# A fused attention and two-layer MoE kernel: another order of VectorE and ScalarE work in its chunk pairs, relu taken with the addition out of PSUM, and weight subtractions on GpSimd

## The chip, the cores and the metric

The kernel runs on one core of a Trainium2 chip. The metric is the device time of one execution in microseconds (us): the median of several runs. A core has five engines that each take their instructions strictly in order: TensorE (PE; its weight loads are shown apart as PEld), VectorE (DVE), ScalarE (ACT), GpSimd (POOL) and SyncE (SP), which here only starts transfers.

## The reference, cut to what matters

Attention over clusters comes first; its output, 1536 tokens of 512 values, goes through two dense layers with 2048 hidden values each. The change concerns the two layers.

```python
def _moe_ref(x, w_in, w_out):
    h = x @ w_in
    g = h * (1.0 / (1.0 + np.exp(-1.702 * h)))
    return (g @ w_out).astype(np.float32)

def _moe2_ref(x, w_in, w_out):
    h = x @ w_in
    r = np.maximum(h, 0.0)
    g = r * r
    return (g @ w_out).astype(np.float32)

    # reference: q, k, v are (2, 8, 768, 64), the weights 64-bit floats
    x = np.ascontiguousarray(attn_out.transpose(0, 2, 1, 3)).reshape(B * S, H * D)
    x = _moe_ref(x=x, **moe_kwargs)
    return _moe2_ref(x=x, **moe2_kwargs)
```

## The kernel before, in words

**Numbers.** Every matrix operand is split into a high part (a ScalarE cast to the short matmul format) and a low part (the rest, by a VectorE subtraction), and a product is three products of parts: high by high, high by low, low by high. The weights arrive as 64-bit floats and are decoded into 32-bit ones: ScalarE takes the magnitude of the high word (L81), then VectorE does four instructions, L90, L92, L95 and L98 (`decode`); the last two read two tiles each. `parts` (L102) splits a decoded weight tile into `hi` and `lo`.

**Order.** The program's order is written out by hand (`manual_schedule`): each engine executes its instructions in the order in which the code issues them, and an instruction that waits holds back everything behind it on its engine.

**Attention** takes the first 300 us and a little more. Towards its end the first weights of layer 0 are decoded beside it. Each head group ends in a normalization by GpSimd (L501, 128x768).

**Chunk loop** (L884 to L941): layer 0 for the first batch half, 16 chunks of 128 hidden values. For each chunk TensorE does `hidden` (into PSUM tile `ph`) and then `second` of the chunk before (into `y`). Beside this, the next chunk's two weight tiles (`wi` from w_in, `oh`/`ol` from w_out) are loaded, decoded and split. Two raw tiles alternate between w_in and w_out: a new load (L72, L75) can start only when the last decoding step has read the raw tile. The decoded weights are also stored in DRAM (`keep`, L122) for the second batch half.

**Chunk pairs** (L951 to L1071): 24 of them in three passes of eight: layer 0 for the second batch half, layer 1 for the first, layer 1 for the second. Each pair multiplies a block of two chunks and carries `second` of the pair before in four quarters (`pend[0]` to `pend[3]`). The first three pairs are plain: four units, each with a product into PSUM (L839), a gate (sigmoid on ScalarE, multiplication on VectorE, L701), a cast `gh` (L982) and a subtraction `gl` (L984). The other 21 do seven products of sums in place of eight (L832). TensorE's order in these is: B11, B21, `pend[0]`, T2, T1, `pend[1]`, T3, B22, `pend[2]`, T4, `pend[3]`. Two PSUM tiles alternate, so T1 needs the first addition (L1016) done, T4 the additions L1045 and L1047, and the next pair's second product the gate behind T4. Between them VectorE and ScalarE prepare the next pair's weights: `sums` (four additions or subtractions, L799 to L802), `early` (casts L805 and subtractions L806 of `wxh`/`wxl`), `late` (`wyh`/`wyl`). At pass boundaries the combinations of the tokens (`Combos.sum`, L776, and `Combos.part`, L783 and L784) and the copies of finished outputs (`finish`, L747) come on top.

**Layer 1's weights** are decoded inside the pairs of the first two passes, up to four tiles per pair by the table `COUNTS`; `do(i, steps)` places steps 0 to 3 (the four decoding instructions) and 4 (storing or splitting) of the pair's i-th tile. In layer 1 the gate is `gated` (L710, a maximum and a multiplication in one VectorE instruction) or, for the last quarter, a ScalarE relu and a VectorE multiplication (L703, L704); then a cast (L695) and a subtraction (L696).

Of the kernel before, what the change touches and what calls it, by code (L numbers as in the profile page):

```python
# [20 lines left out]
BIG = float(2**40)  # L21

# [9 lines left out]
def tile_kernel(ctx, tc, q, k, v, cent, w_in1, w_out1, w_in2, w_out2, cw_cols, out):  # L32
# [665 lines left out]
    def gate(layer, dst, src, tmp):  # L698
        if layer == 0:
            nc.scalar.activation(tmp, src, ACTF.Sigmoid, scale=1.702)  # L700
            nc.vector.tensor_mul(dst, src, tmp)  # L701
        else:
            nc.scalar.activation(tmp, src, ACTF.Relu)  # L703
            nc.vector.tensor_mul(dst, tmp, tmp)  # L704

    def gated(layer, dst, tmp):
        if layer == 0:
            gate(layer, dst, dst, tmp)
        else:
# [76 lines left out]
    class Weights:  # L786
# [56 lines left out]
    COUNTS = (2, 4, 4, 2, 2, 2, 2, 1, 1, 2, 2, 2, 2, 2, 2, 0)  # L843
# [17 lines left out]
    def step(k):  # L861
# [22 lines left out]
    for fc in range(KF):  # L884
# [15 lines left out]
        def act(i):  # L900
            gate(0, s[:, cut[i]], first[i] if fc == 0 else hidden(xs, w, i), s[:, cut[i]])
# [49 lines left out]
    for q, (layer, b, p) in enumerate(slots):  # L951
# [22 lines left out]
        if q < NC:  # L974
            xq = [[x[i] for i in r] for r in ((0, 1), (7, 6))]
            for c, g in ((0, ga), (1, gb)):
                for i, at in enumerate((lo_, hi_)):
                    plain(bank[i], wq.x, c, xq[i])
                    gate(0, h[:, c, at], bank[i], s[:, at])
                    if 2 * c + i < n:  # L980
                        absolute()
                    nc.scalar.copy(g[0][:, at], h[:, c, at])  # L982
                    do(2 * c + i, (0, 1))
                    nc.vector.tensor_sub(g[1][:, at], h[:, c, at], f32(g[0][:, at]))  # L984
                    do(2 * c + i, (2, 3, 4))
                    if i:
# [122 lines left out]
```

## Time and profile before

| | us |
|---|---|
| median of 3 runs | 814.11 (812.75 to 814.85) |
| the profiled execution | 813.53 |
| its span in the trace | 811.7 |
| TensorE busy | 784.2, 97% |
| VectorE busy | 666.0, 82% |
| ScalarE busy | 478.2, 59% |
| GpSimd busy | 121.9, 15% |

The span runs from the first to the last instruction that the profiler recorded. Busy shares are means over stages with different limits; which wait ends last in a stage is read from the stage's own rows. A timeline row has its start in us, its length, engine, line, operation, output and input tile with shapes, a count where equal ones are taken together, and in brackets how long the engine stood idle before it and what ended that. TensorE's granted clock is given as a share of its upper level: 1.00 is 2.4 GHz, 0.50 is 1.2 GHz.

### The profile page before, as it was taken

The numbers are of one execution on the slowest core, as the hardware profiler recorded it, in microseconds if no ns is written. First come the engines' busy times: TensorE is split into PE (matmuls) and PEld (weight loads), VectorE is DVE, ScalarE is ACT, GpSimd is POOL, SyncE is SP. The second block draws the span as 40 slices with busy tenths as digits, with TensorE's granted clock in tenths as the row PEclk, the third lists the DMA queues.
The fourth block names the chain that finished last, engine by engine and source line by source line (L and its number), as shares of the span: only waits on it lengthen the run. The fifth ranks groups of instructions, "written<-read, shape, count | busy, mean of one in ns | idle before, by whom it ended". The sixth has DMA issues, their size and how long they took to land.

```text
span 811.7 us, 12557 instructions
## 1 busy us (share of the span) xinstructions
PE 784.2 (97%) x4521; PEld 697.9 (86%) x4521; DVE 666.0 (82%) x1202; ACT 478.2 (59%) x1004; POOL 121.9 (15%) x121
## 2 busy tenths in 40 slices
PE   8999999999999999999999899989999999999997
PEld 5898889999988887788899789977998887998986
DVE  7899999998898787878888898888888987656653
ACT  5898888988988644444564545556354545433331
POOL 1444435545436100000000000000000000000000
PEclk9999999999999999999999899999999999999999
DMA  8342533532311344445436533312342301300002
GB/s 229 89 132 63 160 105 90 138 89 66 83 26 34 88 153 142 149 142 178 157 107 205 155 92 116 131 53 64 118 155 80 104 26 40 117 27 26 27 1 78
DMA packets 48478, 81.87 MB, mean 101 GB/s; under 512 B 5120, under 2 KB 32544, under 8 KB 48416
## 3 DMA queue, kind: packets, MB, share of 16 engines
q1 hardware_dynamic: 43232, 73.96, 30.5%
q10 hardware_dynamic: 5184, 7.12, 2.7%
q8 instruction: 35, 0.57, 0.3%
q14 instruction: 27, 0.22, 0.1%
HBM read 58.76 MB, written 11.58 MB: 87 GB/s over the span
## 4 chain that ended last, share of the span: by engine, by line
PE 52%; DVE 27%; ACT 10%; DMA 5%; issue 4%; POOL 1%; ACTq 0%; SPq 0%; DVEq 0%; POOLq 0%
PE ps L832 12%; PE y L727 12%; PE pa L453 5%; PE pt L428 5%; DMA raw<-in_moe_w_in_dram 4%; PE ph L140 4%; PE y L721 3%; PE ps L404 3%; DVE el L441 3%; DVE dec L98 2%; DVE nm L410 2%; PE ps L405 2%; DVE dec L95 2%; DVE wxl L806 2%; PE y L723 2%
## 5 line engine op out<-in xcount | busy, mean ns | idle before, releaser
L695 ACT CAST gh<-h 128x384 fp32r<-128x384 f32 (+1 forms) x63 | 39.1, 621 | 109.9 <-DVE h L710 82.2
L441 DVE TENSOR_TENSOR el<-pt,eh 128x384 fp32r<-128x384 f32 x192 | 97.5, 549 | 7.6 <-ACT eh L438 7.3
L410 DVE TENSOR_REDUCE nm<-ps 128x1 f32<-128x768 f32 x96 | 91.2, 950 | 11.9 <-PE ps L405 11.0
L419 ACT ACTIVATE e<-ps,nm 128x768 f32<-128x768 f32 x96 | 88.7, 924 | 16.9 <-DVE nm L410 9.6
L438 ACT CAST eh<-pt 128x384 fp32r<-128x384 f32 x192 | 84.2, 497 | 8.5 <-PE pt L428 7.5
L428 PE MATMUL pt<-identF,e 128*128 128x128 f32 x576 | 82.2, 276 | 3.3 <-DVE el L441 2.8
L832 PE MATMUL ps<-x,wxh 128*128 128x384 f32 x336 | 74.4, 343 | 5.5 <-ACT wxh L805 2.9
L727 PE MATMUL y<-oh,gl 128*128 128x512 f32 x192 | 75.9, 395 | 0.0
L727 PE MATMUL y<-ol,gh 128*128 128x512 f32 x192 | 75.8, 395 | 0.0
L727 PE MATMUL y<-oh,gh 128*128 128x512 f32 x192 | 74.6, 389 | 0.0
L428 PEld LDWEIGHTS pt<-identF,e 128*128 128x128 f32 x576 | 64.4, 140 | 9.6 <-DVE el L441 8.9
L404 PE MATMUL ps<-k,q 80*128 80x512 f32 x192 | 70.3, 366 | 0.5 <-ACT k L371 0.5
L696 DVE TENSOR_TENSOR gl<-h,gh 128x384 fp32r<-128x384 f32 (+1 forms) x63 | 43.5, 691 | 32.7 <-ACT gh L695 32.7
L81 ACT ACTIVATE dec<-raw 128x512 f32<-128x512 f32 x64 | 43.1, 673 | 45.0 <-DMA raw<-in_moe_w_out_dram 15.9
L832 PEld LDWEIGHTS ps<-x,wxh 128*128 128x128 f32 x336 | 59.9, 191 | 11.0 <-ACT wxh L805 3.2
L405 PE MATMUL ps<-k,q 128*128 128x512 f32 x192 | 61.2, 340 | 0.0
L832 PE MATMUL ps<-x,wyh 128*128 128x384 f32 x252 | 55.3, 340 | 5.7 <-DVE h L1045 5.1
L140 PE MATMUL ph<-xh,wi 128*128 128x512 f32 (+1 forms) x256 | 53.7, 342 | 3.3 <-ACT wi L104 3.1
L832 PEld LDWEIGHTS ps<-x,wyh 128*128 128x128 f32 x252 | 44.0, 188 | 11.5 <-DVE h L1045 4.4
L140 PEld LDWEIGHTS ph<-xh,wi 128*128 128x128 f32 x256 | 41.4, 189 | 12.1 <-ACT wi L104 6.6
L721 PE MATMUL y<-gh,ol 128*128 128x512 f32 x128 | 51.0, 399 | 0.0
L721 PE MATMUL y<-gl,oh 128*128 128x512 f32 x128 | 50.8, 397 | 0.0
(170 smaller groups left out, 1896.0 us busy)
## 6 DMA issues: line engine op xcount, KB each, us to landing
raw<-in_moe_w_in_dram SPq DMA_DIRECT2D x32, 512.0 KB, 4.0
raw<-in_moe_w_out_dram SPq DMA_DIRECT2D x32, 512.0 KB, 3.2
wb<-wst SPq DMA_DIRECT2D x24, 512.0 KB, 4.6
wst<-dec SPq DMA_DIRECT2D x32, 256.0 KB, 2.5
k<-k SPq DMA_DIRECT2D x16, 192.0 KB, 4.0
q<-q SPq DMA_DIRECT2D x16, 192.0 KB, 2.9
rr<-row SPq DMA_DIRECT2D x16, 192.0 KB, 3.6
out_dram<-o SPq DMA_DIRECT2D x12, 256.0 KB, 2.0
```

The costliest lines, as they stand in the source:

```text
L140: nc.tensor.matmul(ph, w[:, kc * P:(kc + 1) * P], xs[kc][z][:, a:a + n], start=(j == 0), stop=(j == len(terms) - 1))
L404: nc.tensor.matmul(ps[:, a:a + n], q1[0:K1, qs], k1[0:K1, a:a + n], start=True, stop=False)
L405: nc.tensor.matmul(ps[:, a:a + n], q2[:, qs], k2[:, a:a + n], start=False, stop=True)
L410: nc.vector.tensor_reduce(out=nm, in_=live["s", t][:, 0:S], op=ALU.max, axis=AX, negate=True)
L419: nc.scalar.activation(e, live["s", t][:, 0:S], ACTF.Exp, bias=live.pop(("nm", t)), accum_out=sums[:, s:s + 1])
L428: nc.tensor.transpose(pt[:, i], e[:, kc * P:(kc + 1) * P], identF)
L438: nc.scalar.copy(place("eh", t, u), live["pt", t, u])
L441: nc.vector.tensor_tensor(out=place("el", t, u), in0=live.pop(("pt", t, u)), in1=f32(place("eh", t, u)), op=ALU.subtract)
L696: nc.vector.tensor_sub(gl[:, at], src[:, at], f32(gh[:, at]))
L721: nc.tensor.matmul(y[m], l[:, cs], r[:, 0:512], start=first, stop=last)
L727: nc.tensor.matmul(y[m], l[:, m * P:(m + 1) * P], r, start=(fc == 0 and z == 0), stop=(fc == KF - 1 and z == 2))
L832: nc.tensor.matmul(ps, w[a][:, wi, kc * P:(kc + 1) * P], x[z][:, kc, :], start=start and j == kc == 0, stop=j == 2 and kc == 1, skip_group ...
```

## The change

1. `parts` does its subtraction on GpSimd, but for the w_out tiles of layer 1, which stay on VectorE.
2. In layer 1 the addition out of PSUM, the maximum with 0 and a minimum with the largest float are one VectorE instruction (`TENSOR_ADD_SAT`, in `total`). ScalarE then squares twice (`squared`): once into the high part, once in place; VectorE subtracts (`low`).
3. In a pair, the additions stand ahead of the next weights' `sums`, and the second half of `early` comes behind the last gate or at the pair's end. The combinations of tokens have other places (`EXTRA` for the plain pairs).
4. `COUNTS` changes: the first and third pair 2 and 4 become 3 and 3; the eighth pair does no decoding (1 before), the sixteenth one (0 before).

```diff
-    def parts(tf, hi, lo):
+    def parts(tf, hi, lo, engine=nc.gpsimd):
         nc.scalar.copy(hi, tf)
-        nc.vector.tensor_tensor(out=lo, in0=tf, in1=f32(hi), op=ALU.subtract)
+        engine.tensor_tensor(out=lo, in0=tf, in1=f32(hi), op=ALU.subtract)
...
+    def total(layer, dst, ps, other):
+
         if layer == 0:
+            nc.vector.tensor_tensor(out=dst, in0=ps, in1=other, op=ALU.add)
         else:
+            nc.vector._custom_dve(TENSOR_ADD_SAT, out=dst, in0=ps, in1=other, s0=TOP, s1=0.0)
+
+    def low(g, c, at):
+        nc.vector.tensor_sub(g[1][:, at], h[:, c, at], f32(g[0][:, at]))
+
+    def squared(g, c, at):
+        nc.scalar.activation(g[0][:, at], h[:, c, at], ACTF.Square)
+        nc.scalar.activation(h[:, c, at], h[:, c, at], ACTF.Square)
...
-    COUNTS = (2, 4, 4, 2, 2, 2, 2, 1, 1, 2, 2, 2, 2, 2, 2, 0)
+    COUNTS = (3, 4, 3, 2, 2, 2, 2, 0, 1, 2, 2, 2, 2, 2, 2, 1)
+    EXTRA = ((((0, 0),), ((0, 1),)), (((0, 2), (1, 4)), ((0, 3), (1, 2))), (((1, 5),), ()))
...
-                parts(tf, *wo2[fc])
+                parts(tf, *wo2[fc], nc.vector)
...
-        nc.vector.tensor_tensor(out=h[:, 0, lo_], in0=B_, in1=p1, op=ALU.add)
-        do(0, (0, 1))
-        gated(layer, h[:, 0, lo_], s[:, lo_])
+        total(layer, h[:, 0, lo_], B_, p1)
+        if layer == 0:
+            nc.scalar.activation(s[:, lo_], h[:, 0, lo_], ACTF.Sigmoid, scale=1.702)
+            do(0, (0, 1))
+            nc.vector.tensor_mul(h[:, 0, lo_], h[:, 0, lo_], s[:, lo_])
+            nc.scalar.copy(ga[0][:, lo_], h[:, 0, lo_])
+        else:
+            squared(ga, 0, lo_)
+            do(0, (0, 1))
...
-        if q + 1 < len(slots):
-            wn.sums()
-            wn.early()
+        if more:
+            wn.early(0)
...
-        nc.vector.tensor_tensor(out=h[:, 1, lo_], in0=B_, in1=u2, op=ALU.add)
-        do(1, (2, 3))
-        gated(layer, h[:, 1, :], s)
-        do(1, (4,))
-        split(gb, h[:, 1, :])
+        total(layer, h[:, 1, lo_], B_, u2)
+        if layer == 0:
+            nc.scalar.activation(s, h[:, 1, :], ACTF.Sigmoid, scale=1.702)
+            if more:
+                wn.sums()
+            nc.vector.tensor_mul(h[:, 1, :], h[:, 1, :], s)
+            nc.scalar.copy(gb[0], h[:, 1, :])
+        else:
+            squared(gb, 1, slice(0, S))
+            if more:
+                wn.sums()
+        do(1, (2,))
+        low(gb, 1, slice(0, S))
...
+        if more and n < 2:
+            wn.early(1)
+        do(1, (3,))
+        low(ga, 0, hi_)
+        if more and n > 1:
+            wn.early(1)
+        do(1, (4,))
```

The rows below are instructions in the order in which an engine takes them. VectorE in the chunk loop, one chunk, before (`s` is the gate, `wi` and `ol` the low parts of the two weight tiles, `dec` the decoded tile):

```order
L701 TENSOR_TENSOR s<-ph,s 128x256
L105 TENSOR_TENSOR wi<-dec,wi 128x512
L95 SCALAR_TENSOR_TENSOR dec<-raw_5025,dec 128x512
L696 TENSOR_TENSOR gl<-s,gh 128x256
L98 SCALAR_TENSOR_TENSOR dec<-raw_5025,dec 128x512
L105 TENSOR_TENSOR ol<-dec,oh 128x512
L90 TENSOR_SCALAR dec<-dec 128x512
L92 TENSOR_SCALAR dec<-dec 128x512
L95 SCALAR_TENSOR_TENSOR dec<-raw_5066,dec 128x512
L98 SCALAR_TENSOR_TENSOR dec<-raw_5066,dec 128x512
```

The same place after the change:

```order
L699 TENSOR_TENSOR gl<-s,gh 128x512
L703 TENSOR_TENSOR s<-ph,s 128x256
L98 SCALAR_TENSOR_TENSOR dec<-raw_5025,dec 128x512
L699 TENSOR_TENSOR gl<-s,gh 128x256
L101 SCALAR_TENSOR_TENSOR dec<-raw_5025,dec 128x512
L93 TENSOR_SCALAR dec<-dec 128x512
L95 TENSOR_SCALAR dec<-dec 128x512
L98 SCALAR_TENSOR_TENSOR dec<-raw_5066,dec 128x512
L101 SCALAR_TENSOR_TENSOR dec<-raw_5066,dec 128x512
```

The two subtractions have left VectorE; the lines are three further down in the changed file, so that L98 and L101 there are the two last decoding steps.

GpSimd in the loop's first chunks after the change (before, it took only the normalization, the last row of L501):

```order
L108 TENSOR_TENSOR wi<-dec,wi 128x512
L108 TENSOR_TENSOR ol<-dec,oh 128x512
L108 TENSOR_TENSOR wi<-dec,wi 128x512
L108 TENSOR_TENSOR ol<-dec,oh 128x512
L504 TENSOR_TENSOR x_1_86<-x_1_86,rr 128x768
L108 TENSOR_TENSOR wi<-dec,wi 128x512
L108 TENSOR_TENSOR ol<-dec,oh 128x512
```

GpSimd has two subtractions for each chunk now, and the last head group's normalization (L504 there) stands behind the fourth `ol`, inside the loop.

VectorE in the first plain pair, from the second unit's gate to the next pair's weights, before (`h` is a unit's gate):

```order
L776 TENSOR_TENSOR x_1_86<-x_1_86 128x2x384
L701 TENSOR_TENSOR h<-ps,s 128x384
L984 TENSOR_TENSOR gl<-h,gh 128x384
L701 TENSOR_TENSOR h<-ps,s 128x384
L984 TENSOR_TENSOR gl<-h,gh 128x384
L806 TENSOR_TENSOR wxl<-wb,wxh 128x512
```

After:

```order
L783 TENSOR_TENSOR x_1_86<-x_1_86 128x2x384
L703 TENSOR_TENSOR h<-ps,s 128x384
L93 TENSOR_SCALAR dec<-dec 128x512
L95 TENSOR_SCALAR dec<-dec 128x512
L713 TENSOR_TENSOR gl<-h,gh 128x384
L98 SCALAR_TENSOR_TENSOR dec<-raw_5328,dec 128x512
L101 SCALAR_TENSOR_TENSOR dec<-raw_5328,dec 128x512
L703 TENSOR_TENSOR h<-ps,s 128x384
L713 TENSOR_TENSOR gl<-h,gh 128x384
L813 TENSOR_TENSOR wxl<-wb,wxh 128x512
```

A whole decode (L93, L95, L98, L101) now stands between the third unit's gate and the fourth's.

VectorE in the first pair of the last pass, from a token part to the additions in front of T4, before (`o` is a finished output):

```order
L784 TENSOR_TENSOR x_7587<-x_0_85,x_7586 128x768
L799 TENSOR_TENSOR wt<-wb 128x256
L800 TENSOR_TENSOR wt<-wb,wt 128x256
L801 TENSOR_TENSOR wt<-wb 128x256
L802 TENSOR_TENSOR wt<-wb,wt 128x256
L806 TENSOR_TENSOR wxl<-wb,wxh 128x512
L806 TENSOR_TENSOR wxl<-wt,wxh 128x512
L784 TENSOR_TENSOR x_7589<-x_1_86,x_7588 128x768
L747 COPY o<-y_6717 128x512
L1045 TENSOR_TENSOR h<-ps,p_4018 128x384
```

After:

```order
L791 TENSOR_TENSOR x_7590<-x_0_85,x_7589 128x768
L791 TENSOR_TENSOR x_7586<-x_1_86,x_7585 128x768
L813 TENSOR_TENSOR wxl<-wb,wxh 128x512
L754 COPY o<-y_6705 128x512
L710 ISA h<-ps,p_4018 128x384
L710 ISA h<-ps,p_5033 128x384
L806 TENSOR_TENSOR wt<-wb 128x256
L807 TENSOR_TENSOR wt<-wb,wt 128x256
L808 TENSOR_TENSOR wt<-wb 128x256
L809 TENSOR_TENSOR wt<-wb,wt 128x256
```

The four sums and the second subtraction of `wxl` no longer stand in front of the additions, which are the custom instruction (ISA, L710) there.

## Rows read from the trace of the kernel before

**Rows 1.** Page, part 1: busy us, share, instructions of each engine.

```profile
PE 784.2 (97%) x4521; PEld 697.9 (86%) x4521; DVE 666.0 (82%) x1202; ACT 478.2 (59%) x1004; POOL 121.9 (15%) x121
```

**Rows 2.** TensorE's waits from 300 us: us in total, times, longest us.

```profile
PE ps L832 <- DVE h L1045: 5.1, 5, 1.7
PE ph L140 <- ACT wi L104: 3.1, 4, 1.7
PE ps L832 <- ACT wxh L805: 2.9, 1, 2.9
PE ps L832 <- DVE h L1016: 1.5, 3, 0.6
...
PE ps L832 <- DVE wxl L806: 0.5, 1, 0.5
```

**Rows 3.** TensorE's timeline: two chunk starts, the first plain pair's start.

```profile
297.71 0.40 PE L140 MATMUL ph<-xh,wi 128*128 128x512 f32 x1
...
306.13 0.40 PE L140 MATMUL ph<-xh,wi 128*128 128x512 f32 x1
...
404.64 0.34 PE L839 MATMUL ps<-x,wxh 128*128 128x384 f32 x1
```

**Rows 4.** TensorE's timeline: starts of chunk pairs.

```profile
417.46 0.44 PE L839 MATMUL ps<-x,wxh 128*128 128x384 f32 x1 [0.18 <-DVE h L701]
...
453.88 0.69 PE L832 MATMUL ps<-x,wxh 128*128 128x384 f32 x1 [2.85 <-ACT wxh L805]
...
490.44 0.34 PE L832 MATMUL ps<-x,wxh 128*128 128x384 f32 x1
...
506.05 0.34 PE L832 MATMUL ps<-x,wxh 128*128 128x384 f32 x1
...
522.39 0.34 PE L832 MATMUL ps<-x,wxh 128*128 128x384 f32 x1
...
559.53 0.34 PE L832 MATMUL ps<-x,wxh 128*128 128x384 f32 x1
...
689.39 0.51 PE L832 MATMUL ps<-x,wxh 128*128 128x384 f32 x2
...
705.10 0.33 PE L832 MATMUL ps<-x,wxh 128*128 128x384 f32 x1
```

**Rows 5.** Busy us by engine (instructions), PEclk, DMA share, GB/s, one stretch.

```profile
core 0: us, PE busy (x) PEld busy (x) DVE busy (x) ACT busy (x) POOL busy (x), PEclk, DMA share, GB/s
453.90:460.50 6.60, 6.12 (x18) 5.32 (x19) 6.53 (x13) 4.35 (x8) 0.00 (x0) 0.50 0.94 302
```

**Rows 6.** Timelines of ScalarE and VectorE in one chunk.

```profile
346.45 0.66 ACT L81 ACTIVATE dec<-raw 128x512 f32<-128x512 f32 x1 [1.99 <-DMA raw<-in_moe_w_in_dram]
...
347.66 0.69 DVE L105 TENSOR_TENSOR ol<-dec,oh 128x512 fp32r<-128x512 f32 x1 [1.50 <-ACT oh L104]
...
349.91 0.69 DVE L98 SCALAR_TENSOR_TENSOR dec<-raw,dec 128x512 uint32<-128x512 uint32 x1
```

**Rows 7.** Timelines of GpSimd and VectorE in attention.

```profile
126.11 1.01 POOL L385 TENSOR_TENSOR v<-rawv,v 128x384 fp32r<-128x384 f32 x1
126.30 1.36 DVE L98 SCALAR_TENSOR_TENSOR dec<-raw,dec 128x512 uint32<-128x512 uint32 x1
...
253.65 1.83 POOL L501 TENSOR_TENSOR x<-x,rr 128x768 f32<-128x768 f32 x1
```

**Rows 8.** VectorE's timeline: gates in the first and third plain pair.

```profile
415.26 0.55 DVE L701 TENSOR_TENSOR h<-ps,s 128x384 f32<-128x384 f32 x1
...
449.16 0.55 DVE L701 TENSOR_TENSOR h<-ps,s 128x384 f32<-128x384 f32 x1
...
452.21 0.55 DVE L701 TENSOR_TENSOR h<-ps,s 128x384 f32<-128x384 f32 x1
```

**Rows 9.** VectorE's timeline: first pair of the last pass.

```profile
681.36 0.42 DVE L799 TENSOR_TENSOR wt<-wb 128x256 f32<-128x256 f32 x1
...
685.50 0.55 DVE L1045 TENSOR_TENSOR h<-ps,p 128x384 f32<-128x384 f32 x1
```

**Rows 10.** Page, part 5: ScalarE's casts of gates, busy us, mean ns.

```profile
L695 ACT CAST gh<-h 128x384 fp32r<-128x384 f32 (+1 forms) x63 | 39.1, 621 | 109.9 <-DVE h L710 82.2
```

More of the change, by code (lines that the diff above doesn't have):

```diff
@@ L8 @@
 from concourse._compat import with_exitstack
+from concourse.dve_ops import TENSOR_ADD_SAT
 from concourse.masks import make_identity
@@ L21 @@
 BIG = float(2**40)
+TOP = float(np.finfo(np.float32).max)
 E_LO = float(np.uint32(0x38000000).view(np.float32))
@@ L900, in act @@
         def act(i):
-            gate(0, s[:, cut[i]], first[i] if fc == 0 else hidden(xs, w, i), s[:, cut[i]])
+            gate(s[:, cut[i]], first[i] if fc == 0 else hidden(xs, w, i), s[:, cut[i]])
         act(0)
@@ L991, in tile_kernel @@
                             wn.plain(c, wq.x)
-                            combos.sum(2 * q + c)
                         elif not c:
                             wn.sums()
-                            combos.part(4)
                         else:
-                            wn.early()
-                            combos.part(2)
+                            wn.early(0)
+                            wn.early(1)
+                        for kind, j in EXTRA[q][c]:
+                            (combos.part if kind else combos.sum)(j)
+                    do(u, (4,))
             wo = wo1
@@ L1004, in tile_kernel @@
             continue
+        last = p == NP - 1 and q + 1 < len(slots)
+        more = q + 1 < len(slots)
         product(A, wq.x, wq.B11, x[Combos.A11], True)
@@ L1041, in tile_kernel @@
         do(1, (0, 1))
-        if p == NP - 1 and q + 1 < len(slots):
-            nxt.part(2)
         product(A, wq.y, wq.T3, x[Combos.S3])
-        nc.vector.tensor_tensor(out=h[:, 1, hi_], in0=A, in1=p5, op=ALU.add)
+        total(layer, h[:, 1, hi_], A, p5)
         product(B_, wq.y, wq.B22, x[Combos.S4])
-        nc.vector.tensor_tensor(out=h[:, 1, lo_], in0=B_, in1=u2, op=ALU.add)
-        do(1, (2, 3))
-        gated(layer, h[:, 1, :], s)
-        do(1, (4,))
-        split(gb, h[:, 1, :])
+        total(layer, h[:, 1, lo_], B_, u2)
[5 more added lines that the diff above has]
+            nc.scalar.copy(gb[0], h[:, 1, :])
+        else:
+            squared(gb, 1, slice(0, S))
[3 more added lines that the diff above has]
+        low(gb, 1, slice(0, S))
+        if last:
+            nxt.part(3)
         pend[2]()
@@ L1054, in tile_kernel @@
         product(A, wq.y, wq.T4, x[Combos.A22])
-        gate(layer, h[:, 0, hi_], A, s[:, hi_])
-        split(ga, h[:, 0, :], hi_)
+        if layer == 0:
+            gate(h[:, 0, hi_], A, s[:, hi_])
+            nc.scalar.copy(ga[0][:, hi_], h[:, 0, hi_])
+        else:
+            nc.scalar.activation(h[:, 0, hi_], A, ACTF.Relu)
+            squared(ga, 0, hi_)
+        if more and n < 2:
[3 more added lines that the diff above has]
+        if more and n > 1:
+            wn.early(1)
+        do(1, (4,))
         if q < 2 * NP and p > 3:
@@ L1060, in tile_kernel @@
             nxt.sum(p - 4)
-        if p == NP - 1 and q + 1 < len(slots):
-            nxt.part(3)
+        if last:
             nxt.part(4)
```

56 lines of the change are left out of this document (25 added, 31 removed).

## The prediction

> **What bounds the kernel now.** Three views, in this order. The page's engine shares first [rows 1]: TensorE is busy 97% of the span, VectorE 82%, ScalarE 59%, GpSimd 15%. The change leaves TensorE's instructions as they are, so all that can be won is the time in which it stands or runs at half clock. Then its waits from 300 us on [rows 2]: VectorE's adds and ScalarE's casts are what it waits for. Last, the starts of its groups, which tell what a stretch loses against the same stretch undisturbed; I count by these, since a halted TensorE loses more than the wait that is written beside it.
>
> - Chunk loop [rows 3]: one chunk without a stall takes 306.13 − 297.71 = 8.42. The eleven up to 404.64 take 98.51 against 92.62: 5.9 lost.
> - Chunk pairs [rows 4]: layer 0 takes 506.05 − 490.44 = 15.61 per undisturbed pair, layer 1 705.10 − 689.39 = 15.71. Against these: the opening loses 2.85 ahead of 453.88 and then 36.56 − 31.22 = 5.34 up to 490.44. Of that 5.34, 3.3 is the clock: from 453.9 to 460.5, right behind the 2.85 in which TensorE stood, the granted clock is 0.50, the lower of its levels [rows 5], so half of 6.6 us went. Then 0.73 (506.05 to 522.39, 16.34 long), 5.92 (522.39 to 559.53, two pairs with the first pass boundary), and 4.18 (559.53 to 689.39, eight pairs with the second boundary). Behind 689.39 nothing is lost.
>
> So some 19 us are lost in the pairs and 5.9 in the chunk loop. The profiled run was 813.53, its span 811.7 (1.8 lies outside the span); the median of the runs shown is 814.11, 0.6 above. The sum is made against 813.53.
>
> **Part 1: the subtraction of `parts` goes from VectorE to GpSimd.** What sets the chunk's period is a ring [rows 6]: a raw tile lands, ScalarE takes its magnitude at 346.45, casts `oh`, VectorE waits for that cast and subtracts (347.66), decodes in four instructions until 349.91 + 0.69 = 350.60, and the raw tile is free for its next load. With the subtraction gone from VectorE, L90 and L92 can start when the magnitude is done (346.45 + 0.66 = 347.11) and end at about 348.0; before they ended near 349.1. But GpSimd then subtracts beside VectorE. In attention a decode's L98 that began at 126.30 took 1.36, not its usual 0.69, beside a GpSimd subtraction of 1.01 that ended at 127.12, and was done 0.54 after that end [rows 7]. GpSimd takes 1.01 for 384 columns and 1.83 for 768, so some 1.28 for 512 (estimate, by line between the two). If it starts at 348.0, it holds until 349.3; L95 is done 0.55 later at 349.85, L98 0.7 later at 350.55: the same as the 350.60 of before. Price per chunk: 0, between −0.7 (no hindrance: VectorE is freed of the 0.69) and +1.3 (the whole GpSimd time comes on top). I take 0, since the row of 126.30 is the same instruction against the same kind of neighbour.
>
> The Trainium skill ("SBUF — State Buffer", section "Who interferes with whom") says that a VectorE instruction with two SBUF inputs contends with a GpSimd instruction that reads SBUF, and that the one which issues first holds the shared pair for its whole length while the other fully blocks. The row at 126.30 agrees that the hindrance ends with the GpSimd instruction; taken literally the waiting instruction would then need all of its 0.69 where the row shows 0.54, and the sum would be 0.15 × 11 = 1.7 higher.
>
> One instruction more is moved by this: GpSimd's 128x768 normalization of the last head group (L501), which ran beside attention's end, now stands behind the fourth `ol` subtraction, so it falls into the loop, between L95 and L98 of a chunk. It takes 1.83 [rows 7]: cost between 0 (falls where VectorE waits) and 1.84. I take **+1.0**, the middle, there being no row for it.
>
> **Part 2: opening, plain pairs.** Counts of decodes in the first pairs go from 2, 4, 4 to 3, 4, 3. A plain unit with a decode takes VectorE 452.21 − 449.16 = 3.05 from its gate to the next [rows 8]. The first pair's third unit (gate at 415.26) now carries one, so the fourth unit's gate starts at 415.26 + 3.05 = 418.31 and ends at 418.86. The next pair's second product needs it and started at 417.46 [rows 4]: about **+1.4**, a new stall. The third pair loses a decode behind its last gate but starts 1.4 later; its last gate lands near 453.5 where it was 452.21, and the pair's casts and the first product behind it near 455.2. So the stall of 2.85 stays about as long, and with it the clock's 3.3. What goes is behind it: the 0.5 for `wxl` [rows 2], and 1.5, the rest of the 5.34 (5.34 − 3.3 − 0.5), waits for adds that no longer stand behind the sums and casts of the next weights. Together +1.4 − 0.5 − 1.5 = **−0.6**.
>
> **Part 3: order within a pair.** Before, four sums and both halves of `wxl` stand ahead of the adds (L1045, L1047) on VectorE; in the last pass's first pair 4.14 us lie between the first sum at 681.36 and the add at 685.50, and TensorE waits for the add [rows 9]. Now the sums stand behind the adds and the second half of `wxl` behind the gate. They are the same instructions, covered by the fourth product and the fourth quarter of `second`; without that cover they would cost their length, at 0.42 a sum 1.7. The 5.1 on L1045 and 1.5 on L1016 [rows 2] thus go: **−0.7** (506.05), **−5.9** at the first boundary. At that boundary one thing is late next: with no decode in the pair ahead, `gl` of the last quarter stands behind ScalarE's cast and VectorE's second `wxl`, some 1.3 later than before, and the next pair's first quarter reads it: I leave **+1.1** there (0 to 1.3). Layer 1 with its boundary gets **−4.0** of the 4.18; 0.2 is kept for the same wait.
>
> The decode that leaves the eighth pair for the sixteenth, and the x-combinations taken earlier, cost nothing on VectorE: it is 82% busy, and behind 522.39 it has the sums' room; without it, one decode is 2.25 (from 347.66 + 0.69 to 350.60 [rows 6]).
>
> **Part 4: relu with the add, squares on ScalarE.** No row shows the new add (add, max 0, min). It reads PSUM and SBUF like the add of 0.55 at 685.50 [rows 9]; the bounds are 0.42, a sum of 256 columns, and 1.36, the slowest decode row [rows 7]. I take 0.55, the same operands. At the upper bound three adds cost a pair 2.4 more, of which VectorE gets back the three multiplies that it loses, so even then nothing is late by more than some tenths. ScalarE does two squares where VectorE did one instruction and ScalarE one cast; the cast is 0.62 [rows 10], 39 us for 63. One more per group: covered, ScalarE being 59% busy; uncovered it would be 0.6 on the wait for `gl`, again inside the +0.2 and the rival below. Cost 0.
>
> **Sum.** 0 + 1.0 − 0.6 − 0.7 − 5.9 + 1.1 − 4.0 = −9.1, so 813.53 − 9.1 = **804.4**.
>
> **Rivals.**
> - *GpSimd's subtractions don't hinder VectorE.* Then VectorE's ring is 0.7 shorter per chunk, TensorE's 8.42 becomes the period, the 5.9 of the loop goes, and the normalization's 1.0 does too: 804.4 − 6.9 = 797.5. For it: only one instruction pair of the trace is against it. Against: that row is the very decode step that the ring ends with. 0.17.
> - *Slower: GpSimd lengthens the ring.* If each subtraction (1.28, two per chunk, of which one on the ring) comes on top of the decode instead of beside the wait, eleven chunks pay 1.28 each: +14.1, 818.5. It outweighs the gain of 10.1 elsewhere once a chunk's ring grows by more than 0.9. For it: two of the four decode steps read two tiles as the hindered L98 did. Against: ahead of 347.66 VectorE stood for 1.50 [rows 6], time that the new order hands back. 0.11.
> - *The stalls of the pairs only move*: to `gl` behind the second `wxl`, and to ScalarE's squares. If half of the 9.6 gained at the boundaries and in layer 1 comes back, 809.2. For it: TensorE takes products and `second` in a fixed order and four buffers of `gh`/`gl` leave little room. Against: VectorE's and ScalarE's idle time. 0.14.
> - *The opening's stall shortens enough that the clock stays at its upper level.* Then 3.3 more goes: 801.1. For it: a decode less in the third pair; against: the 1.4 lost ahead. 0.14.
> - Forecast 0.40; anything else 0.04.
>
> **How the numbers follow.** A measurement of this kernel can tell about 0.3%, 2.4 us, from no change. Faster: forecast, first, third and fourth rival, less the third's upper tail and the unknown rest: 0.79. Within: 0.10, from the third's tail and smaller forms of the second. Slower: 0.11. The range takes in the first rival's 797.5 with a us for the unknown add, and the third's 809.2 with 1.8 for the unhidden norm: 796.5 to 811.0; left out are the slower rival and most of the rest.
>
> **What would show it.** In the changed profile: a wait of about 1.6 on the fourth gate ahead of the second plain pair; one of about 2.9 with a clock of 0.50 behind it near 455; no wait above 0.3 on the adds at the boundaries, about 1.1 on `gl` at layer 1's first pair; L98 rows of 1.3 to 1.4 beside GpSimd rows near 1.28; the eleven chunks 98 to 101 long. The prediction is wrong if the chunks take less than 95 or more than 103, or if a boundary still loses over 2.

## The result and the profile after

The changed kernel takes 802.25 us (median of 4 runs, 800.09 to 803.57) against 814.48 for the kernel before on the same chip (812.75 to 816.35): a ratio of 0.9847, 95% interval 0.9816 to 0.9878. The profiled execution took 803.57, its span is 800.6. The forecast of 804.4 and its range held, but several of its steps were wrong, and errors of both signs cancelled: that the sum came so near is in part luck.

The engines' shares of the changed kernel, as in [rows 1]:

```profile
PE 778.6 (97%) x4520; PEld 697.6 (87%) x4521; DVE 645.2 (81%) x1122; ACT 507.5 (63%) x1052; POOL 163.7 (20%) x153
```

VectorE gave up 20.8 us of busy time, ScalarE took 29.3 more, GpSimd 41.8 more. That tells little yet; the waits and the starts do. TensorE's waits from 290 us on (as [rows 2]: us in total, times, longest):

```profile
PE ph L143 <- ACT wi L107: 3.4, 4, 1.5
PE ps L840 <- ACT wxh L812: 2.7, 1, 2.7
PE ps L847 <- DVE h L703: 2.4, 1, 2.4
PE y L728 <- DVE gl L713: 0.9, 1, 0.9
PE ps L840 <- DVE h L710: 0.6, 1, 0.6
```

The waits of 5.1 and 1.5 for additions are down to 0.6 (L710); those for the loop's cast (3.4) and for `wxh` (2.7) are as they were; the 2.4 on the gate L703 is new. TensorE's starts, answering to [rows 3, 4] with the places in the same order; ahead of them is the start of the chunk that stood at 280.87 before (two chunks of 8.42 ahead of 297.71):

```profile
279.02 0.40 PE L143 MATMUL ph<-xh,wi 128*128 128x512 f32 x1
...
402.81 0.34 PE L847 MATMUL ps<-x,wxh 128*128 128x384 f32 x1
...
417.81 0.44 PE L847 MATMUL ps<-x,wxh 128*128 128x384 f32 x1 [2.36 <-DVE h L703]
...
454.09 0.69 PE L840 MATMUL ps<-x,wxh 128*128 128x384 f32 x1 [2.72 <-ACT wxh L812]
...
486.76 0.34 PE L840 MATMUL ps<-x,wxh 128*128 128x384 f32 x1
...
502.36 0.34 PE L840 MATMUL ps<-x,wxh 128*128 128x384 f32 x1
...
517.96 0.34 PE L840 MATMUL ps<-x,wxh 128*128 128x384 f32 x1
...
551.49 0.34 PE L840 MATMUL ps<-x,wxh 128*128 128x384 f32 x1
...
678.25 0.33 PE L840 MATMUL ps<-x,wxh 128*128 128x384 f32 x1
```

Differences of neighbouring starts, in us, for all kernels that were run. The columns: **start** of that chunk; the **14 chunks** from it to the first plain pair; the three **plain** pairs; the two pairs behind, **opening**; the next **two** pairs; **boundary 1** with the eighth and ninth pair; the eight pairs of **layer 1** with the second boundary. Undisturbed, the 14 chunks would take 14 × 8.42 = 117.88, opening, two and boundary 1 31.22 each, and layer 1 125.68. (Attention's last products end at 268.97 in the kernel before, and not at 300.)

| kernel | start | 14 chunks | plain | opening | two | boundary 1 | layer 1 |
|---|---|---|---|---|---|---|---|
| before | 280.87 | 123.77 | 49.24 | 36.56 | 31.95 | 37.14 | 129.86 |
| changed | 279.02 | 123.79 | 51.28 | 32.67 | 31.20 | 33.53 | 126.76 |
| e1_parts_vector | 281.16 | 122.84 | 51.94 | 31.34 | 31.20 | 33.52 | 126.76 |
| e2_loop_vector | 279.45 | 125.64 | 51.95 | 31.34 | 31.21 | 33.53 | 126.75 |
| e3_norm_early | 278.14 | 122.44 | 51.50 | 32.87 | 31.20 | 33.54 | 126.75 |
| e4_memset | 278.64 | 117.88 | 51.99 | 31.35 | 31.20 | 33.52 | 126.76 |
| e5_old_counts | 278.90 | 124.51 | 49.13 | 34.54 | 31.20 | 37.32 | 125.63 |
| e6_old_relu | 278.09 | 125.79 | 51.69 | 31.37 | 31.20 | 34.11 | 130.75 |
| e7_before_relu | 281.89 | 122.40 | 49.15 | 37.03 | 31.91 | 36.51 | 128.54 |
| e8_counts_243 | 280.07 | 125.57 | 49.14 | 32.77 | 31.20 | 36.27 | 126.78 |
| e9_before_parts | 278.50 | 123.96 | 49.50 | 37.26 | 31.93 | 37.21 | 129.90 |
| e10_before_counts | 280.22 | 123.48 | 51.90 | 33.22 | 31.91 | 36.18 | 130.79 |
| e11_ol_later | 278.71 | 118.42 | 51.82 | 31.36 | 31.20 | 33.51 | 126.75 |
| e12_ol_later_counts | 279.97 | 118.00 | 48.94 | 32.88 | 31.20 | 33.54 | 126.74 |

The span became 11.1 shorter: 1.85 in attention, 0 in the chunks, 1.85 in plain pairs and opening together, 0.75, 3.61 and 3.10. The last columns repeat to some hundredths wherever the code is the same; the 14 chunks do not. The same loop took 123.8 to 125.8 in five kernels, so a difference under 2 us there is not read from one profile.

Some entries hold a stretch in which TensorE's clock was granted at 0.50 to 0.51 for some 3.5 us; each such stretch costs 1.7. There is one in the plain pairs or the opening of every row (in the opening of before, e5, e7 and e9 it is twice as long and costs 3.4), one in boundary 1 of e5 and of e8, one in layer 1 of e6, and one in attention, near 21 us, in e2, e7, e8 and e12. Where one of them bears on a comparison, it is said there.

### The profile page after: what moved, and what is told of

It is laid out like the page before. It is cut to its first block, busy times and chain, and to the rows that moved or that the text cites. A ratio compares the mean times of both kernels' runs of the same rounds, so it can differ in the third digit from the quotient of the medians.

```text
span 800.6 us, 12533 instructions
## 1 busy us (share of the span) xinstructions
PE 778.6 (97%) x4520; PEld 697.6 (87%) x4521; DVE 645.2 (81%) x1122; ACT 507.5 (63%) x1052; POOL 163.7 (20%) x153
## 4 chain that ended last, share of the span: by engine, by line
PE 58%; DVE 17%; DMA 12%; ACT 8%; issue 2%; POOL 1%; ACTq 0%; SPq 0%; POOLq 0%; DVEq 0%
PE ps L840 16%; PE y L734 15%; DMA raw<-in_moe_w_in_dram 6%; PE pa L456 5%; PE pt L431 5%; DMA raw<-in_moe_w_out_dram 3%; PE y L728 3%; PE ps L407 3%; DVE el L444 3%; PE ps L408 2%; DVE dec L98 2%; DVE nm L413 2%; DVE dec L101 2%; ACT dec L84 2%; DMA wst<-dec 2%
## 5 line engine op out<-in xcount | busy, mean ns | idle before, releaser
L716 ACT ACTIVATE gh<-h 128x384 fp32r<-128x384 f32 (+1 forms) x48 | 30.4, 633 | 72.5 <-DVE h L710 72.0
L98 DVE SCALAR_TENSOR_TENSOR dec<-raw,dec 128x512 uint32<-128x512 uint32 x64 | 70.0, 1093 | 0.8
L713 DVE TENSOR_TENSOR gl<-h,gh 128x384 fp32r<-128x384 f32 (+1 forms) x75 | 50.0, 667 | 22.9 <-ACT h L717 19.6
```

Source lines behind the costliest of these rows:

```text
L98: nc.vector.scalar_tensor_tensor(out=t, in0=high, scalar=0xC0000000, in1=t, op0=ALU.bitwise_and, op1=ALU.bitwise_or)
```

## The experiments: GpSimd's subtractions

**All subtractions back on VectorE** (e1)

```diff
-    def parts(tf, hi, lo, engine=nc.gpsimd):
+    def parts(tf, hi, lo, engine=nc.vector):
```

> The changed kernel with every subtraction of parts back on VectorE. Theory: GpSimd's subtractions gain only in attention, where VectorE no longer stands 0.81 us for ScalarE's cast ahead of its own subtraction, twice; so attention is about 1.9 longer again (chunk loop from 297.7 where the changed kernel has 295.9), the sixteen chunks behind it stay near 107 us, and the time is near 804.2. Rival: the chunk loop was helped by GpSimd; then it is 2 or more longer than 107 and the time over 805. Other rival: the loop was hurt; then it is below 105 and the time under 802.

Measured: 803.88 us, ratio to before 0.988 (0.9865 to 0.9895). The chunk starts at 281.16, 2.1 later than in the changed kernel, and the 14 chunks take 122.84, within the loop's own spread. Attention's part of the theory holds; the loop gained nothing from GpSimd.

**Only the loop's on VectorE (e2); and GpSimd's subtractions alone in the kernel before (e9)**

```diff
-            parts(tf, new[0], new[1])
+            parts(tf, new[0], new[1], nc.vector)
...
-                parts(tf, new[2], new[3])
+                parts(tf, new[2], new[3], nc.vector)
```

> The changed kernel with the subtractions of the chunk loop back on VectorE and only the two inside attention on GpSimd. Theory: attention as in the changed kernel (loop stretch begins near 295.9), the loop stretch 106.9 as in both kernels, time near 802.3. Rival, that GpSimd's subtractions hurt the loop: 105 or less, 800.5. Rival, that they helped: 109 or more.

The other run takes item 1 of the change, and nothing else, into the kernel before:

```diff
-    def parts(tf, hi, lo):
+    def parts(tf, hi, lo, engine=nc.gpsimd):
...
-        nc.vector.tensor_tensor(out=lo, in0=tf, in1=f32(hi), op=ALU.subtract)
+        engine.tensor_tensor(out=lo, in0=tf, in1=f32(hi), op=ALU.subtract)
...
-                parts(tf, *wo2[fc])
+                parts(tf, *wo2[fc], nc.vector)
```

> The kernel before with only the subtractions of parts put on GpSimd. Theory: attention about 1.9 shorter, the loop stretch unchanged at 106.9 though L95 of the decoding rises from 0.69 to about 1.65, everything behind it as before: 812.5. Rival: loop helped, under 810; loop hurt, over 814.

Measured: 802.75 (ratio 0.9858, 0.9838 to 0.9878) and 812.27 (0.998, 0.9968 to 0.9993), so the subtractions alone are worth some 2 us of the 12, and that is in attention. The loop took 123.96 in e9, where the kernel before takes 123.77. Over all kernels, the start is 278.1 to 280.1 (mean 278.9, ten kernels) where attention's two subtractions are on GpSimd and 280.2 to 281.9 (mean 281.0, four kernels) where they are on VectorE: 2.1 us. Without the 1.7 that the clock cost e2, e7, e8 and e12 ahead of it, it is 277.7 to 279.0 against 280.2 to 281.2, and the two groups stand well apart.

VectorE's timeline in attention shows why, first of the kernel before, then of the changed one:

```profile
64.13 0.34 DVE L258 CAST nat<-rawk 128x384 fp32r<-128x384 f32 x1
65.28 0.82 DVE L105 TENSOR_TENSOR wi<-dec,wi 128x512 fp32r<-128x512 f32 x1 [0.81 <-ACT wi L104]
66.03 0.94 DVE L410 TENSOR_REDUCE nm<-ps 128x1 f32<-128x768 f32 x1
```

```profile
64.15 0.34 DVE L261 CAST nat<-rawk 128x384 fp32r<-128x384 f32 x1
64.44 0.96 DVE L413 TENSOR_REDUCE nm<-ps 128x1 f32<-128x768 f32 x1
```

Before, VectorE stood 0.81 for ScalarE's cast, then subtracted, and the row maximum queued behind it began at 66.03, not 64.44. Some 1.2 of that reached TensorE, and the same happens once more near 98 us (with `ol`); 0.4 of the two is lost again near 205 us.

**The normalization ahead of the loop** (e3)

```diff
-            if c == 4:
+            if c == 1:
                 last_norm()
```

> The changed kernel with the last 128x768 normalization issued behind the first ol subtraction, so that GpSimd does it near 276, ahead of the loop's critical stretch. Theory: the 2.22 us of one decode step beside it (0.69 usual) falls to 0.69 and the stretch from the chunk start at 295.9 to the first plain pair is 1.5 shorter: 105.4, time near 800.7. Rival: the loop makes it up elsewhere, no change, 802.3.

In the changed kernel the normalization falls on the decode of one chunk, VectorE's and GpSimd's rows:

```profile
300.82 2.29 POOL L504 TENSOR_TENSOR x<-x,rr 128x768 f32<-128x768 f32 x1
301.44 2.22 DVE L101 SCALAR_TENSOR_TENSOR dec<-raw,dec 128x512 uint32<-128x512 uint32 x1
```

Moved ahead (it runs at 273.92), the same step takes 0.69 and the 14 chunks 122.44 against 123.8 to 125.8. The time is 801.61 (0.9852, 0.9835 to 0.987): by the intervals not apart from the changed kernel. The 1.5 is there in the rows, and the stretch agrees with it, but the time does not settle it. The starts of single chunks do. TensorE stands ahead of the chunk behind that step, and the third of the 14 chunks takes 9.9 in place of 8.42:

```profile
295.86 0.40 PE L143 MATMUL ph<-xh,wi 128*128 128x512 f32 x1
...
305.76 0.50 PE L143 MATMUL ph<-xh,wi 128*128 128x512 f32 x1 [1.31 <-ACT wi L107]
```

It took 9.9 to 10.2 in all five kernels that have the normalization there and the subtractions on GpSimd, and 8.4 to 8.8 in the nine others. The eleven chunks behind it took 97.9 on average in those five, and 98.0 in the five kernels with the loop's subtractions on VectorE in their old place. So the normalization costs 1.5 beside these subtractions, and by these averages the subtractions themselves neither gain nor lose.

**A fill in place of the loop's subtraction** (e4)

```diff
+        if engine is None:
+            nc.gpsimd.memset(f32(lo), 0.0)
+            return
         engine.tensor_tensor(out=lo, in0=tf, in1=f32(hi), op=ALU.subtract)
...
-            parts(tf, new[0], new[1])
+            parts(tf, new[0], new[1], None)
```

The loop's other calls of `parts` get the same `None`; the kernel so leaves the low parts of these weights out.

> The changed kernel with the loop's GpSimd subtractions replaced by a GpSimd fill of the same tile, which reads nothing; the low parts of layer 0's first weights are left out of the computation. Theory: the fill does not hold up VectorE, L98 falls from 1.65 to 0.69, each chunk's ring from 8.5 to about 7.6, below TensorE's 8.42, and the loop stretch is 102 to 103 (the normalization's 1.5 stays), time near 798. Rival, that loads or ScalarE bound the loop anyway: stretch stays near 107, 802.

Measured: 796.14 (0.9786, 0.977 to 0.9802). The 14 chunks take 117.88, which is 14 × 8.42: no stall is left. The decoding step L98, grouped over the loop (count, busy us, mean ns), beside GpSimd's subtraction in the changed kernel, and with the fill:

```profile
L98 DVE SCALAR_TENSOR_TENSOR dec<-raw,dec 128x512 uint32<-128x512 uint32 x22 | 36.2, 1646 | 0.4
```

```profile
L98 DVE SCALAR_TENSOR_TENSOR dec<-raw,dec 128x512 uint32<-128x512 uint32 x22 | 15.1, 685 | 0.4
```

One chunk of the changed kernel, answering to [rows 6]:

```profile
344.79 0.67 ACT L84 ACTIVATE dec<-raw 128x512 f32<-128x512 f32 x1 [2.32 <-DMA raw<-in_moe_w_in_dram]
...
345.50 0.43 DVE L93 TENSOR_SCALAR dec<-dec 128x512 f32<-128x512 f32 x1 [0.84 <-ACT dec L84]
...
346.05 1.49 POOL L108 TENSOR_TENSOR ol<-dec,oh 128x512 fp32r<-128x512 f32 x1 [2.88 <-ACT oh L107]
...
346.42 1.66 DVE L98 SCALAR_TENSOR_TENSOR dec<-raw,dec 128x512 uint32<-128x512 uint32 x1
348.12 0.69 DVE L101 SCALAR_TENSOR_TENSOR dec<-raw,dec 128x512 uint32<-128x512 uint32 x1
```

GpSimd ends at 347.54, L98 at 348.08, 0.54 later, as in attention [rows 7]. From the magnitude's start to the end of the last step it is 4.02 (344.79 to 348.81), before 4.15. The subtraction that left VectorE comes back as L98's length. The same 0.54 to 0.55 stands behind GpSimd's end at every L98 of the loop that meets a subtraction.

The fill is not the same neighbour without its reading. It does not wait for ScalarE's cast, so it runs earlier, beside L93, L95 and `gl`, and L98 finds GpSimd idle. Nor does it hold up nothing: where it stands beside L95, as at 350.49, L95 takes 0.71 in place of 0.43. So the run shows what the loop takes once L98 is free of GpSimd, and that neither loads nor ScalarE bound it; what a fill would do to L98 it does not show.

## The experiments: the table of decodes

**Old table in the changed kernel (e5); 2, 4, 3 with one in the eighth pair (e8); the new table alone in the kernel before (e10)**

```diff
-    COUNTS = (3, 4, 3, 2, 2, 2, 2, 0, 1, 2, 2, 2, 2, 2, 2, 1)
+    COUNTS = (2, 4, 4, 2, 2, 2, 2, 1, 1, 2, 2, 2, 2, 2, 2, 0)
```

> The changed kernel with the table of decodes of before (2, 4, 4 in the plain pairs, 1 in the eighth pair, 0 in the sixteenth). Theory: the 2.36 us stall ahead of the second plain pair goes; behind the third pair the decode delays the second half of wxl again, TensorE halts twice and the clock stays at 0.50 for some 6.6 us instead of 3.1; the first pass boundary is about 1 longer. Sum: first plain pair to the third product pair (83.95 us in the changed kernel) near 84.3, time near 803.5. Rival: only the stall goes, 800.

```diff
-    COUNTS = (3, 4, 3, 2, 2, 2, 2, 0, 1, 2, 2, 2, 2, 2, 2, 1)
+    COUNTS = (2, 4, 3, 2, 2, 2, 2, 1, 1, 2, 2, 2, 2, 2, 2, 1)
```

> The changed kernel with 2, 4, 3 decodes in the plain pairs and the one taken away put back into the eighth pair. Theory: the 2.36 us stall ahead of the second plain pair goes and nothing takes its place (the stall of 2.7 and the half clock behind the third pair stay as they are), so that stretch is 2.2 shorter; the first boundary gets 0.5 to 1.3 longer by its decode. Time 800.6 to 801.4. Rival: the stall moves to the third pair's end, 802.3 or more.

```diff
-    COUNTS = (2, 4, 4, 2, 2, 2, 2, 1, 1, 2, 2, 2, 2, 2, 2, 0)
+    COUNTS = (3, 4, 3, 2, 2, 2, 2, 0, 1, 2, 2, 2, 2, 2, 2, 1)
```

> The kernel before with the changed table of decodes alone. New theory: the decode that leaves the eighth pair gives the first boundary's gain, in either order: its stretch falls from 37.1 to near 34; the plain pairs get 2 longer (49.2 to 51.3) by the decode in the first, the last boundary's stretch about 1 longer (131) by the decode in the sixteenth pair; time 813 to 814. Rival, the order is needed for it: 37 stays, 816.

Measured: 805.57 (0.9898, 0.988 to 0.9915), 803.17 (0.9856, 0.9827 to 0.9885) and 812.86 (0.9997, 0.9978 to 1.0017).

- The third decode in the first plain pair costs the plain pairs 2.1 to 2.9 in either order (51.3 to 52.0 against 48.9 to 49.5), up to 1.7 of it by the clock; plain pairs and opening together show 1.4 (81.82 in e12, 83.18 in e11) to 2.0 (81.91 in e8, 83.95 in the changed kernel). The theory held; the forecast's price was 1.4.
- The decode in the eighth pair costs boundary 1 2.7 to 3.8 in the new order (36.27 and 37.32 against 33.53): much more than the "about 1" or "0.5 to 1.3" expected, which was a miss. 1.7 of it is the clock. With that decode TensorE stands 1.5 for a gate (L703) and 0.9 for `gl` some 2 us later, and the clock falls behind the second; in the changed kernel the gate costs 0.3, the 0.9 is the same, and the clock stays. Less the clock the decode costs 1.0 (e8) and 2.1 (e5). TensorE's waits at boundary 1 with the old table, and in the changed kernel:

```profile
PE ps L840 <- DVE h L703: 1.5, 1, 1.5
PE y L728 <- DVE gl L713: 0.9, 1, 0.9
PE ps L840 <- ACT p L1046: 0.7, 1, 0.7
```

```profile
PE y L728 <- DVE gl L713: 0.9, 1, 0.9
PE ps L840 <- DVE h L703: 0.3, 1, 0.3
PE ps L840 <- DVE x L791: 0.2, 1, 0.2
```

  The clock there (granted share behind the counts) in e5 and in e8:

```profile
540.50:544.00 3.50, 3.50 (x11) 3.00 (x12) 3.47 (x7) 1.65 (x4) 0.00 (x0) 0.51 0.03 7
539.80:543.30 3.50, 3.46 (x11) 2.97 (x12) 3.47 (x6) 1.65 (x5) 0.00 (x0) 0.51 0.02 5
```

- The new table alone gains 1.0 there (36.18 against 37.14); with the new order as well 3.0 (34.11 in e6, with the old arithmetic). So at the new table the order is worth 2.1. At the old table it is worth nothing: with the new arithmetic in both, the old order takes 36.51 (e7) and the new one 37.32 (e5), since the clock's 1.7 takes more than the order gives. The arithmetic of layer 1 gives 0.6 in either order (37.14 to 36.51, 34.11 to 33.53). The expectation that the table does it in either order fell.
- The decode in the sixteenth pair costs layer 1 0.9 to 1.1 (126.76 against 125.63; 130.79 against 129.86).

## The experiments: order and arithmetic in layer 1

**The old arithmetic in the new order (e6), and the new arithmetic in the old order (e7)**

```diff
-            nc.vector._custom_dve(TENSOR_ADD_SAT, out=dst, in0=ps, in1=other, s0=TOP, s1=0.0)
+            nc.vector.tensor_tensor(out=dst, in0=ps, in1=other, op=ALU.add)
...
-        nc.scalar.activation(g[0][:, at], h[:, c, at], ACTF.Square)
-        nc.scalar.activation(h[:, c, at], h[:, c, at], ACTF.Square)
+        nc.vector.scalar_tensor_tensor(out=h[:, c, at], in0=h[:, c, at], scalar=0.0, in1=h[:, c, at],
+                                       op0=ALU.max, op1=ALU.mult)
+        nc.scalar.copy(g[0][:, at], h[:, c, at])
```

> The changed kernel's order with layer 1's arithmetic as before: plain addition, maximum and multiplication in one VectorE instruction, one cast on ScalarE. Theory: the order gave layer 1's gain, so layer 1's stretch of eight pairs with the second boundary stays near 126.8 (129.9 before) and the time near 802.3. Rival: the arithmetic gave it, stretch near 129.9, 805.4.

The other way round, `total` and both squares are put into the kernel before with its order left alone:

```diff
-        nc.vector.tensor_tensor(out=h[:, 1, lo_], in0=B_, in1=u2, op=ALU.add)
+        total(layer, h[:, 1, lo_], B_, u2)
...
-        gated(layer, h[:, 1, :], s)
+        if layer == 0:
+            gated(layer, h[:, 1, :], s)
         do(1, (4,))
-        split(gb, h[:, 1, :])
+        (squared if layer else split)(gb, h[:, 1, :])
```

> The kernel before, in its own order, with layer 1's new arithmetic alone (addition with relu in one VectorE instruction, two squares on ScalarE). New theory, after the run with the old arithmetic in the new order: the arithmetic gives layer 1's gain by taking instructions off VectorE; the stretch of eight pairs with the second boundary falls from 129.9 to 126.5 or less, the first boundary (37.1) by 0.5, time near 810. Rival: order and arithmetic are only worth something together; the stretch stays above 129, 813.5. Theory of the prediction: order alone; same as the rival.

Measured: 806.41 (0.9913, 0.9888 to 0.9939) and 811.2 (0.9969, 0.9956 to 0.9983). Layer 1 took 130.75 and 128.54. TensorE's waits in that stretch with the old arithmetic, then with the new arithmetic in the old order, then in the changed kernel:

```profile
PE ps L841 <- DVE h L710: 1.3, 2, 1.1
PE ps L841 <- ACT p L1047: 0.7, 1, 0.7
PE ps L841 <- ACT p L1023: 0.5, 1, 0.5
```

```profile
PE ps L846 <- DVE h L712: 1.5, 2, 1.1
```

```profile
PE ps L840 <- DVE h L710: 0.6, 1, 0.6
```

Compared at the same table: the new table with the old arithmetic takes 130.79 in the old order and 130.75 in the new one, so in these two executions the order alone gives nothing. But 1.7 of the 130.75 is the clock again, which fell behind two waits that the old arithmetic leaves, 0.53 ahead of 668.47 and 1.09 ahead of 670.88; neither the old order nor the changed kernel has such a stretch there:

```profile
671.30:674.80 3.50, 3.50 (x12) 3.04 (x11) 1.31 (x3) 3.25 (x7) 0.00 (x0) 0.51 0.21 77
```

So the order takes 1.7 of standing out, and the clock takes it back. The arithmetic alone gives 1.3 (129.86 to 128.54), and the order on top of it 2.9 (to 125.63, which is the undisturbed 125.68). Both theories as they were set fell: neither order nor arithmetic brings the stretch near 126 alone, both together do. The expectation of 126.5 for the arithmetic alone was a miss. No run has the new order with both the old table and the old arithmetic.

## The experiments: a version that beats both

The loop's ring holds two delays: VectorE's wait for a cast before, GpSimd's hindrance after. Both go if VectorE keeps the subtraction but does it behind the next tile's decode (e11; the loop's other subtractions go to VectorE as in e2):

```diff
+        for lo, src, hi in owed:
+            nc.vector.tensor_tensor(out=lo, in0=src, in1=f32(hi), op=ALU.subtract)
+        owed = []
         g = g_tiles()
...
             if c > 1:
-                parts(tf, new[2], new[3])
+                nc.scalar.copy(new[2], tf)
+                owed.append((new[3], tf, new[2]))
```

> The changed kernel with the loop's subtractions on VectorE, the one for ol behind the next tile's four decoding steps in place of ahead of them. Theory: VectorE no longer waits for ScalarE's cast inside the ring and GpSimd holds up nothing; the ring is some 1.1 shorter than the 8.75 of before, below TensorE's 8.42; thirteen chunks take 109.5, where all kernels with the subtraction take 114 to 117.4; time near 796. Rival: VectorE's own work per chunk, which is 0.69 more twice than with the fill, still bounds it: 112 or more, 799 or more.

The second run (e12) adds another table:

```diff
-    COUNTS = (3, 4, 3, 2, 2, 2, 2, 0, 1, 2, 2, 2, 2, 2, 2, 1)
+    COUNTS = (2, 4, 3, 2, 2, 2, 2, 0, 2, 2, 2, 2, 2, 2, 2, 1)
```

> The run with ol later, and the plain pairs' decodes 2, 4, 3 with the one taken away put into the ninth pair, the first behind the pass boundary (2 there, 0 in the eighth). Theory: plain pairs 49.1 in place of 51.3 to 52, boundary stretch 33.5 stays or grows by up to 1; time 794 to 795. Rival: the ninth pair's decode costs the boundary as much as the eighth's did (2.7 or more): 797 or more.

Measured: 796.48 (ratio to before 0.9797, 0.9777 to 0.9817) and 795.07 (0.9782, 0.9763 to 0.9801). The interval of the second lies below that of the changed kernel (0.9816 to 0.9878), that of the first just touches it. The 14 chunks take 118.42 and 118.00, near the undisturbed 117.88, so GpSimd's hindrance is what kept the changed kernel's loop above it. VectorE's rows of a chunk of the first:

```profile
340.25 0.42 DVE L93 TENSOR_SCALAR dec<-dec 128x512 f32<-128x512 f32 x1
340.70 0.43 DVE L95 TENSOR_SCALAR dec<-dec 128x512 uint32<-128x512 uint32 x1
341.16 0.69 DVE L98 SCALAR_TENSOR_TENSOR dec<-raw,dec 128x512 uint32<-128x512 uint32 x1
341.89 0.69 DVE L101 SCALAR_TENSOR_TENSOR dec<-raw,dec 128x512 uint32<-128x512 uint32 x1
342.50 0.69 DVE L908 TENSOR_TENSOR ol<-dec,oh 128x512 fp32r<-128x512 f32 x1
```

The magnitude began at 339.47, so the raw tile is free after 3.11 (at 342.58) where it took 4.15 before. That last step, the table, is worth little by time: plain pairs 48.94 in place of 51.82, but opening 32.88 in place of 31.36. Boundary 1 stays at 33.54 with two decodes in the ninth pair; the rival that it costs as much there as in the eighth fell.

## Why the prediction was right, and where it was not

- **The loop, 0.** Right, by its own mechanism: the hindrance ends 0.54 behind GpSimd's end, and the ring is 4.02 against the 4.15 of [rows 6]. The forecast had L98 rows of 1.3 to 1.4; they took 1.65. That does not follow from its own working, which has this step start at 348.0 and end at 349.85. In the trace GpSimd's subtraction of `ol` took 1.49, not 1.28, and L98 began 0.37 behind its start; that of `wi` took 1.29, but L98 often began only 0.07 behind its start. The first rival, no hindrance, is excluded: L98 takes 1.65 beside GpSimd's subtractions and 0.69 where VectorE does them (the rows of e11); what the rival promised (5.9) is what e4 gained. The Trainium skill's rule in "SBUF — State Buffer" ("Who interferes with whom") agrees in all but the remainder: the waiting instruction needed 0.54 behind the release, not its whole 0.69. The slower rival counted the whole 1.28 and left out that the wait for the cast goes.
- **The normalization, +1.0.** Measured 1.5, by the third of the 14 chunks; one step took 2.22 in place of 0.69. The 1.83 of [rows 7] is another head group's; the moved one ran at 276.02 for 2.37 before, in the loop's first chunks and not beside attention, and at 300.82 for 2.29 after. That the 14 chunks of the two profiles differ by 0 all the same is the loop's own spread.
- **Attention, no term at all, measured −1.9.** The step that failed is that Part 1 looked for VectorE's wait on the cast in the loop only. The same line has two instances in attention, and there VectorE's queue is what TensorE waits for.
- **Opening, −0.6, measured −1.85.** The new stall was sized 1.4 from [rows 8]; it added 2.0. The decode itself waited 0.63 for ScalarE's magnitude, which the spacing of a pair that was already full does not show:

```profile
414.61 0.43 DVE L93 TENSOR_SCALAR dec<-dec 128x512 f32<-128x512 f32 x1 [0.63 <-ACT dec L84]
```

  The other way, the clock cost half of the 3.3 allowed: granted 0.53 for 3.2 us in place of 0.50 for 6.6 [rows 5]:

```profile
454.00:457.20 3.20, 3.11 (x10) 3.12 (x11) 3.17 (x6) 2.90 (x7) 0.00 (x0) 0.53 0.98 343
457.20:458.00 0.80, 0.80 (x7) 0.75 (x6) 0.10 (x1) 0.27 (x1) 0.00 (x0) 1.00 0.36 143
```

  Before, TensorE stood again for `wxl` behind the first stall; without the last decode in the third pair that wait is gone, and the level rose earlier. e5 and e8 bear this out: with four decodes in the third pair TensorE stands 2.73 and 0.48 and the clock is low for 6.9 us, with three it stands 2.74 once and the clock is low for 3.4. The fourth rival was half right: half of the clock's loss went, though the stall did not shorten.
- **Boundary 1, −4.8, measured −3.6.** The forecast gave it to the order and called the moved decode free. That is half of the cause: the order is worth 2.1 at the new table, and with the decode left in the eighth pair nothing, since the wait that the decode makes brings the clock down. VectorE, 82% busy over the span, was busy there for 3.47 of 3.50 us (the rows of e5 and e8): the share over the span was taken for slack in a stretch that had none. The 1.1 on `gl` was seen as 0.94. The boundary still loses 2.31, and by the prediction's own sign (a boundary that still loses over 2) it is wrong here.
- **Layer 1, −4.0, measured −3.1.** The size came out near, the cause in part: the order alone takes out 1.7 of standing, which the clock took back in e6, and "Part 4: cost 0" left out that the arithmetic is worth 1.3 alone and 4.0 with the order (130.75 to 126.76, 1.7 of it the clock). Of the 0.9 that is missing, the sixteenth pair's decode took all, another that was called free. A wait of 0.6 on an addition is left at the second boundary, over the 0.3 that the prediction allowed. The new addition itself was sized right: 0.555 on average (48 of them, 548 to 558 ns).
- **The two pairs at 490.44 to 522.39, −0.7.** Measured −0.75; all kernels with the new order have it, whatever else they have, so here the order alone did it.

The sum of −9.1 against −11.1 in the span is thus −1.9 for attention and some smaller misses that cancel. By the profiled executions it is −10.0 (813.53 to 803.57), as 3.0 lie outside the span where 1.8 did. The third rival's mechanism, stalls that move to `gl` and to other waits, is what remains at boundary 1 (33.53 against 31.22).

## What to carry to other kernels

Taking an instruction off a busy engine helps where that engine's queue held somebody up; if the instruction goes to an engine that hinders the first, ask what stands beside it, and try first to keep it and only move it behind the work that others wait for. A mean busy share is no slack: a "moved" piece of work has to be priced at the stretch it moves to, boundaries above all. Two edits that each take a part of one queue's length may be worth little alone, also because a wait that is left over can bring the clock down and cost the rest, so undo them one at a time and in pairs before crediting one, and look at the granted clock of each stretch that is compared.

## What was not expected of the hardware

- With the same instructions in plain pairs and opening, the clock fell in either of two places. In the changed kernel TensorE stood for 2.36 ahead of 417.81 and the granted clock stayed at 1.00, then 2.72 ahead of 454.09 and it fell to 0.53. In the run with the old arithmetic it stood 2.44 ahead of 418.97 and the clock fell to 0.50, then 1.60 and it stayed:

```profile
419.00:422.00 3.00, 3.00 (x9) 3.00 (x10) 1.09 (x2) 2.44 (x5) 0.00 (x0) 0.50 0.72 172
...
455.60:458.00 2.40, 2.40 (x13) 2.33 (x14) 2.40 (x5) 2.40 (x6) 0.00 (x0) 1.00 0.95 327
```

  Each cost 1.7 in all, and behind a dip at the first stall the second was 1.5 to 1.6, not 2.6 to 2.7, so the two columns of the table add to 83.1 to 84.4 either way for this table of decodes in the new order. The length of the halt alone does not decide it: in e3 TensorE stood even 2.71 ahead of 415.93, and the clock stayed:

```profile
415.90:419.40 3.50, 3.47 (x20) 3.47 (x21) 1.52 (x3) 3.49 (x7) 0.00 (x0) 1.00 0.72 194
```

  Nor is it the same in each execution of one kernel: the four of e8 had mean granted clocks of 0.993 (the profiled one), 1.000, 0.998 and 0.996 and took 806.62, 800.35, 801.98 and 804.36 us. What decides it stays open.
- GpSimd's fill of 128x512 (0.57 for `wi`, 0.73 for `ol` on average) left VectorE's `gl`, which reads two tiles, at 0.67, but L95, which reads one, took 0.71 in place of 0.43 beside it. With the subtraction it was the other way round: L95 kept its 0.43, and L98, which reads two tiles, took 1.65 in place of 0.69.
